# A fused attention and mixture kernel on one core: new orders for all engines, first queries loaded in another shape, and small edits to the softmax and to the last tile

## The chip, the cores and the metric

The kernel runs on one core of one Trainium2 chip, as one program and one launch. Its time is the device time of one execution in microseconds (us); three executions were timed. Besides those, one execution was recorded by the profiler, and every row shown below comes from that one.

A core has five engines, each working through its own list of instructions in order: TensorE (PE in the profile, with its weight loads as PEld), VectorE (DVE), ScalarE (ACT), GpSimd (POOL) and SyncE (SP). SP only issues transfers here; ACT and POOL issue a few of their own.

## The reference

The attention output of four batches is the token matrix of a two-layer network whose activation is a ratio of two polynomials.

```python
k_sum = k.reshape(B, H, nb, 32, D).max(axis=3)           # B=4, H=8, S=768, D=64
v_sum = v.reshape(B, H, nb, 32, D).mean(axis=3)
scores_l = where(|i-j| < 16, scale * q @ k.T, -1e9)      # a band
scores_s = scale * q @ k_sum.T + log(32)                 # one column for each block of 32 keys
a = softmax(concat(scores_l, scores_s))
x = a @ concat(v, v_sum)                                 # -> 3072 tokens x 512
h = x @ w_in                                             # 512 -> 2048
g = (a0 + a1*h + a2*h^2 + a3*h^3) / (1 + |b0|*|h| + |b1|*h^2 + 1e-6)
out = g @ w_out                                          # 2048 -> 512
```

## The kernel before

**The two halves.** The 3072 tokens are 48 windows of 64 queries (`jj`); eight windows make a group of 512 tokens, so there are six groups. A window of queries sees 96 neighbouring keys and 24 block maxima, 120 columns in all. For each window PE makes scores (`sc`), DVE the row maxima (`sm`), ACT the exponentials (`ss`), POOL the division by the row sum, PE a transpose (`pt`, copied to `pts`), and PE the product with the values (`av`), which ACT or DVE splits into a high part `xh` and a rest `xl`. From the third group on, the transposes go through DRAM (`cross`).

**The two layers.** A step is one group and one of 16 slices (`fc`) of the 2048 hidden columns: 96 steps. `h` of a step is 12 products of 128x512 on PE (high and low parts of tokens and weights), then a chain over ACT and DVE (`tq`, `ta`, `tu`) makes the activation's high part `gh` and, by a last product on POOL, its rest `gl`. Three steps later PE multiplies them by the slice of `w_out` into four sums `po`, 12 products again. PE can never do less than these 96 times 24 products.

**The weights.** A slice of both weight matrices arrives as one 1 MB transfer `wr`, 16 in all, and must be cut into a high and a low part before its `h`. `w_split` does this by one of several recipes, a letter in `MODE`: all have a pass of ACT, one of POOL and one of DVE over the raw words. Then mode `c` copies the high part on ACT and subtracts it on DVE; mode `e` copies on ACT, negates on ACT, and adds the raw words by an accumulating transfer that POOL issues.

**The first group.** Its eight windows take their queries from `qres` and keys from `kres`, resident tiles loaded at the start. Their block means of the values (`vs`) are made on PE, by products with a small averaging matrix, from all ten tiles of values of batch 0 (`vr`, `vw`, `vf`, `vlast`); the means are then copied into each window's value tile (`vw<-vs`, `vr<-vw`, `vlast<-vw`), so no `av` can begin before the last value tile has landed. `PATH` says how a window of the first two groups makes its maxima: `A` scales the maxima with a small DVE instruction and lets ACT read the scores from PSUM; `B` subtracts on DVE.

**What sets the order.** Every instruction is written down by one long list, `ORDER`: a token such as `h12` emits a whole step's products, `a5` the next stage of window 5, `w6` the next stage of the split of slice 6, `W6` its load, `P15` a second-layer step, `g12` the next stage of a step's chain. A wrapper (`Kept`) makes each engine follow the text of this list, and since it records every operation, nearly all instructions carry the line 162. `SLOTS` names the buffer of each tile. Transfers of SP and ACT use eight completion counters in turn: the ninth waits until the first has landed. `NWARM` = 6 products on zeros keep PE working until the first scores; `FILL` could add unread products elsewhere, and is empty.

Of the kernel before, what the change touches and what calls it, by code (L numbers as in the profile page):

```python
# [8 lines left out]
F32 = mybir.dt.float32  # L9
# [5 lines left out]
ALU = mybir.AluOpType  # L15
AX = mybir.AxisListType
# [7 lines left out]
P = 128  # L24
# [28 lines left out]
BYDVE = 'C2 C3 C4 C6 X0 X2 X3'  # L53
# [5 lines left out]
SLOTS = {'wm': '1010', 'ta': '01101010101010101010101010101010101010101010101010101010101010101010101010101010101010101101010101', 'tq': '01010101010101010101010101101010101011001010101010101101010101010101011010010101010101010010101010', 'st': '010101010101010101010101', 'gh': '012020120120120120120120120120120120120120120120121021021021021021021021020120120120120120120210210210', 'h': '0101011110101010101010101010101010010110100100101010101011010101001010101001001010110010101011010110101100101010100101010', 'ks': '0101', 'o': '01230130213021301320132013201320132013201', 'gl': '0121021021021021021021021021021021021021021021021021021021021021021021021021021021021021012102102102', 'sm': '012302312031203102310213021301230132103210321023', 'p': '0132103210123012301021302020232132302103013201021212131032010213013010121321202301021310101013020301021302130', 'xl': '0101010', 'a': '010010101001010101110010101010010111010000010010010111100001101111010010001010011011101000100010101010010100010101010101010101010', 'tu': '010101010101010101010101010101010101010101010101010101010101010101010101010101010101010101101010101', 'xh': '0110101', 'pts': '010101011011011010101011010101010101011011010101', 'vs': '01'}  # L59
NROW = 96  # L60
PTP = 'hhhhhhhhaaaaaaaa'
AVP = 'ooooooooaaaaaaaa'
# [6 lines left out]
K1 K0 K3 d1 S d0 K2 d2 B Q0 d3 c Q1 b0 a1 a0 a1 b2 k8 a0 W0 a2 b1 a2 w0 W1 V2 a1 w0 a0 a1 a3 a3 a2 a2 a6 w0 w1 a3 a4 I w1 W2 a3 V6 a2 a4 w2 a0 F w2 k9  # L69
V3 b3 a5 V1 a3 V0 V7 a4 v3 a2 w1 a6 a3 v1 a4 a6 v9 V5 V4 w1 a5 w0 v2 A8 w0 a0 a0 v6 v8 v0 a7 a6 v4 v5 v7 w1 w2 A9 a6 w1 a1 w2 m0 a5 a5 w2 a1 a7 m3 a0  # L70
b4 m4 W3 a4 w0 m1 a0 a3 a0 m7 a7 m6 a4 a1 a5 W5 w3 m2 W4 a1 G a4 a9 a5 a7 V8 a3 w3 a4 a2 a3 a7 a6 a1 w5 m5 a2 w2 a6 a4 W6 a7 w5 w3 a6 a5 a8 a6 a5 a5
A11 a7 w3 a2 a7 a7 w4 w4 w3 w3 h0 a9 w4 h1 w5 n2 w4 n3 g0 g0 w4 g0 a9 L10 q0 q0 g1 g0 g0 q1 n1 q1 a9 n5 n0 w4 g0 n4 a8 w5 a8 w5 a8 h2 V9 w5 g2 M g1 q2
h3 W8 a9 g2 g1 q2 a8 a9 A10 h4 a8 w6 W7 g2 w6 g1 g1 w6 o a8 a9 D10 L13 a8 P3 w6 w6 a8 g2 g2 g1 a9 g3 w8 g2 w6 g4 V10 W9 a9 q3 g3 w8 g3 b5 w7 q3 a11 P4
a11 w9 w7 q4 g4 g3 g3 W10 g3 q4 g4 a10 D13 a11 h5 w7 P5 w9 a10 L11 g4 h6 w8 g5 g4 w8 L12 w10 w7 g4 P6 w9 P7 D11 V11 q5 A13 D12 q5 g6 g5 w9 w10 w7 a10
a11 w7 g5 a10 g6 w8 h7 q6 a11 A12 g5 w9 a11 k13 a10 a10 a11 g5 a11 a10 a10 w8 g6 k12 w9 a11 W11 a10 q6 b6 g5 w10 g6 g6 g7 g7 W12 q7 w11 w10 w10 g6 g7
q7 a13 a13 A14 h8 A15 g7 g8 w12 a12 w11 P8 g7 h9 g8 w12 q8 w10 g7 w11 w11 q8 w12 g9 P9 W15 g9 g8 P10 a12 g8 h10 g8 w12 g8 w11 b7 a12 g9 q9 w11 q9 g9
w12 g10 W13 g9 P11 a15 h11 w12 V12 g9 w15 q10 a15 W14 a13 g10 P12 w13 a12 w13 g10 a13 V13 a14 q10 g10 A17 h12 g11 g11 w13 a13 g10 q11 w13 w13 g11 a12
w14 q11 g10 a15 a13 P13 w13 a14 w14 g11 a12 g12 g11 g11 a13 a13 g12 V15 q12 a13 a15 g12 h13 g13 P14 a14 w14 q12 a15 g13 w14 g12 a15 a14 a12 a14 w14
w14 g12 h14 q13 a12 a14 a12 a15 q13 V14 g12 w15 g14 a14 a15 a14 g13 w15 a15 w15 w15 P15 A16 a14 q14 g14 w15 g13 b8 q14 A18 g13 a17 g14 g13 h15 A19 a17
g14 g14 g15 g15 g15 q15 a16 q15 h16 P16 g14 g16 g15 a16 g15 g16 P17 h17 q16 L21 g15 P18 q16 g16 g16 g17 f0 a17 g16 q17 g16 a17 f0 g17 a16 g17 q17 g17  # L80
# [30 lines left out]
h93 q92 g92 q92 g92 g93 g93 g92 P93 g92 h94 q93 g93 q93 P94 g93 g93 g94 g94 q94 g94 g93 h95 q94 g95 g94 P95 P96 g95 g94 g95 g94 q95 q95 g95 g95 P97  # L111
g95 P98 f5 f5 f5 f5
"""
MODE = 'ccgcacccbceheccc'
NHALF = NT // HQ


@with_exitstack
def tile_kernel(ctx, tc, qw_in, kraw, kwin, vpad, vred, wio, a, b, cmask, cident, cavg, chot, cbias, out):
    nc = tc.nc  # L120
    class Slotted:


        taken = {}

# [639 lines left out]
```

## Time and profile before

| what | value |
|---|---|
| time, median of 3 runs (lowest to highest) | 633.04 us (632.68 to 633.34) |
| time of the profiled execution | 634.05 us |
| its span, first to last instruction | 632.1 us |
| PE busy | 613.5 us, 97% of the span |
| DVE busy | 558.3 us, 88% |
| ACT busy | 453.6 us, 72% |
| POOL busy | 249.5 us, 39% |
| mean granted PE clock | 0.989 |

The profiled execution has 1.95 us around its span and is 1.01 us above the median. Busy time on PE counts overlapped products, so it says where PE had something to do, not how fast it was. [...]

### The profile page before, as it was taken

The numbers are of one execution on the slowest core, as the hardware profiler recorded it, in microseconds if no ns is written. First come the engines' busy times: TensorE is split into PE (matmuls) and PEld (weight loads), VectorE is DVE, ScalarE is ACT, GpSimd is POOL, SyncE is SP. The second block draws the span as 40 slices with busy tenths as digits, with TensorE's granted clock in tenths as the row PEclk, the third lists the DMA queues.
The fourth block names the chain that finished last, engine by engine and source line by source line (L and its number), as shares of the span: only waits on it lengthen the run. The fifth ranks groups of instructions, "written<-read, shape, count | busy, mean of one in ns | idle before, by whom it ended". The sixth has DMA issues, their size and how long they took to land.

```text
span 632.1 us, 12059 instructions
## 1 busy us (share of the span) xinstructions
PE 613.5 (97%) x4188; PEld 492.6 (78%) x4188; DVE 558.3 (88%) x1073; ACT 453.6 (72%) x1007; POOL 249.5 (39%) x350
## 2 busy tenths in 40 slices
PE   8689989999999999999999999999999999999997
PEld 4477768777888888888888888887888888888885
DVE  5889999999888999989998799998978987798795
ACT  2898979877678767775876777777865875765653
POOL 0865465752416424224433233344242352122231
PEclk9599999999999999999999999999999999999999
DMA  8999668712334343334463413244423022100001
GB/s 317 268 335 319 234 207 275 183 47 68 105 118 147 121 138 91 120 99 146 114 200 114 156 49 113 82 136 125 136 80 101 26 84 87 67 0 2 0 1 66
DMA packets 52660, 80.25 MB, mean 127 GB/s; under 512 B 6440, under 2 KB 33736, under 8 KB 50680
## 3 DMA queue, kind: packets, MB, share of 16 engines
q1 hardware_dynamic: 51096, 75.00, 37.4%
q0 software_dynamic: 1280, 4.39, 3.0%
q8 instruction: 33, 0.54, 0.4%
q14 instruction: 27, 0.22, 0.1%
q10 hardware_dynamic: 224, 0.09, 0.1%
HBM read 60.33 MB, written 14.75 MB: 119 GB/s over the span
## 4 chain that ended last, share of the span: by engine, by line
PE 73%; DVE 12%; DMA 5%; ACT 4%; issue 2%; POOL 2%; SPq 1%; POOLq 0%; DVEq 0%; ACTq 0%
PE h L162 33%; PE po L162 33%; DVE tu L162 3%; DVE tq L162 3%; PE sc L162 3%; PE av L162 3%; DMA wr<-in_wio_dram 2%; DMA vr<-in_vpad_dram 2%; ACT ta L162 2%; DVE gh L162 2%; DVE wr L162 1%; POOL ss L162 1%; POOL gl L162 1%; DMA kres<-in_kraw_dram 1%; PE vs L162 1%
## 5 line engine op out<-in xcount | busy, mean ns | idle before, releaser
L162 POOL TENSOR_TENSOR gl<-tu,ta 128x512 fp32r<-128x512 f32 x96 | 132.6, 1382 | 327.5 <-DVE tu L162 221.8
L162 PE MATMUL po<-w,gh 128*128 128x512 f32 x384 | 119.7, 393 | 0.0
L162 PE MATMUL po<-wearly,gh 128*128 128x512 f32 x384 | 119.5, 392 | 0.0
L162 PE MATMUL h<-xh,wearly 128*128 128x512 f32 x384 | 97.1, 392 | 1.3 <-ACT xh L162 1.1
L162 PE MATMUL h<-xh,w 128*128 128x512 f32 x384 | 97.3, 392 | 0.0
L162 POOL TENSOR_SCALAR ss<-ss,sm 128x120 f32<-128x120 f32 x184 | 83.8, 473 | 23.0 <-DVE sm L162 22.3
L162 ACT ACTIVATE ta<-tq,cs 128x512 f32<-128x512 f32 x96 | 69.4, 723 | 31.9 <-DVE tq L162 29.5
L162 DVE SCALAR_TENSOR_TENSOR gh<-tu,cs,ta 128x512 fp32r<-128x512 f32 x96 | 74.8, 782 | 16.2 <-ACT ta L162 12.4
L162 PEld LDWEIGHTS h<-xh,wearly 128*128 128x128 f32 x384 | 71.4, 188 | 17.8 <-DVE tu L162 1.4
L162 PEld LDWEIGHTS h<-xh,w 128*128 128x128 f32 x384 | 71.3, 188 | 16.0 <-DVE tu L162 0.5
L162 PEld LDWEIGHTS po<-wearly,gh 128*128 128x128 f32 x384 | 71.5, 188 | 15.4 <-issue 0.6
L162 PEld LDWEIGHTS po<-w,gh 128*128 128x128 f32 x384 | 71.2, 188 | 15.4 <-issue 0.6
L162 ACT ACTIVATE ta<-h,cs 128x512 f32<-128x512 f32 x95 | 64.8, 682 | 22.1 <-POOL gl L162 21.8
L162 DVE SCALAR_TENSOR_TENSOR tu<-tu,cs,tq 128x512 f32<-128x512 f32 x96 | 74.0, 771 | 3.4
L162 ACT ACTIVATE sq<-h 128x512 f32<-128x512 f32 x72 | 42.0, 583 | 48.4 <-PE h L162 32.3
L162 PE MATMUL po<-wearly,gl 128*128 128x512 f32 x192 | 75.1, 391 | 0.6 <-POOL gl L162 0.6
L162 PE MATMUL po<-w,gl 128*128 128x512 f32 x192 | 75.2, 392 | 0.3 <-POOL gl L162 0.2
L162 ACT ACTIVATE tu<-h,cs 128x512 f32<-128x512 f32 x96 | 74.6, 777 | 0.0
L162 DVE SCALAR_TENSOR_TENSOR tu<-tu,cs,h 128x512 f32<-128x512 f32 x96 | 71.2, 743 | 1.8
L162 DVE SCALAR_TENSOR_TENSOR tq<-tq,gh 128x512 f32<-128x512 f32 x96 | 69.9, 729 | 1.8
L162 DVE TENSOR_TENSOR tu<-tu,h 128x512 f32<-128x512 f32 x96 | 65.1, 678 | 5.3 <-ACT tu L162 5.3
L162 ACT ACTIVATE ta<-ta 128x512 f32<-128x512 f32 x96 | 60.8, 634 | 3.0
(99 smaller groups left out, 903.6 us busy)
## 6 DMA issues: line engine op xcount, KB each, us to landing
wr<-in_wio_dram SPq DMA_DIRECT2D x15, 1024.0 KB, 5.5
cross<-tb SPq DMA_DIRECT2D x32, 256.0 KB, 2.1
vw<-in_vpad_dram SPq DMA_DIRECT2D x42, 192.0 KB, 2.8
kw<-in_kwin_dram SPq DMA_DIRECT2D x40, 192.0 KB, 3.3
out_dram<-o SPq DMA_DIRECT2D x24, 256.0 KB, 2.6
pts<-cross SPq DMA_DIRECT2D x96, 64.0 KB, 2.6
qw<-in_qw_dram SPq DMA_DIRECT2D x40, 128.0 KB, 2.9
kr<-in_kraw_dram SPq DMA_DIRECT2D x12, 384.0 KB, 4.3
```

Of the source, the lines that this page charges most:

```text
L162: out = getattr(self.engine, name)(*args, **kw)
```

## The change

`ORDER`, `SLOTS` and some of the tables that go with it are replaced as a whole. Their texts tell a reader nothing, so two lines of them stand here and the instructions that they produce stand further down.

```diff
-BYDVE = 'C2 C3 C4 C6 X0 X2 X3'
+BYDVE = 'C2 C3 C4 C6 X0 X13 X2 X3 X6'
-AVP = 'ooooooooaaaaaaaa'
+AVP = 'oohoaoooaaaaaaaa'
-MODE = 'ccgcacccbceheccc'
+MODE = 'ccgcaceebcehpccc'
-K1 K0 K3 d1 S d0 K2 d2 B Q0 d3 c Q1 b0 a1 a0 a1 b2 k8 a0 W0 a2 b1 a2 w0 W1 ...
+K1 Q0 K0 K3 S K2 W0 w0 d3 d0 w0 d1 d2 b0 a1 a0 Q1 a1 w0 W1 a1 a0 w0 ...
...
-        sync.dma_start(out=qres[:, lo:hi], in_=qw_in[0, lo:hi].rearrange("j p r q -> p j r q"))
+        sync.dma_start(out=qres[:, lo:hi], in_=qfirst[:, lo:hi])
...
-            first_q(*((0, 4), (4, HPG))[n])
+            first_q(*((0, 2), (2, HPG))[n])
...
-            dve.tensor_reduce(sm[:, 0, :], flat, axis=AX.X, op=ALU.max, negate=True)
+            peak = sc[:, NPAIR * NK:NPAIR * (NK + 1)] if path == "A" else sm[:, 0, :]
+            dve.tensor_reduce(peak, flat, axis=AX.X, op=ALU.max, negate=True)
             if path == "A":
-                dve.tensor_scalar_mul(sm[:, 0, :], sm[:, 0, :], SCALE)
+                dve.tensor_scalar_mul(sm[:, 0, :], peak, SCALE)
...
-        for pr in range(NPAIR):
-            (dve if jj in SSV else gps).tensor_scalar(ss[:, pr, :], ss[:, pr, :], sm[:, 1, pr:pr + 1], 1.0, op0=ALU.mult, op1=ALU.mult)
+        if jj in SSV:
+            dve.tensor_tensor(ss, ss, sm[:, 1, :].unsqueeze(2).broadcast_to((P, NPAIR, NK)), op=ALU.mult)
+        else:
+            for pr in range(NPAIR):
+                gps.tensor_scalar(ss[:, pr, :], ss[:, pr, :], sm[:, 1, pr:pr + 1], 1.0, op0=ALU.mult, op1=ALU.mult)
...
-            if mode in "cda":
-                dve.tensor_tensor(wt[:, 1, s], w, wt[:, 0, s], op=ALU.subtract)
+            if mode in "cdap":
+                (gps if mode == "p" else dve).tensor_tensor(wt[:, 1, s], w, wt[:, 0, s], op=ALU.subtract)
...
-        gps.tensor_tensor(gl, tu, ta, op=ALU.mult)
+        (dve if (g, fc) == (NG - 1, NFC - 1) else gps).tensor_tensor(gl, tu, ta, op=ALU.mult)
...
+            if g == NG - 1 and t == TPG - 1:
+                half = slice(0, DM // 2), slice(DM // 2, DM)
+                act.copy(o[:, half[0]], pos[g][t][:, half[0]])
+                act.dma_start(out=rows[:, half[0]], in_=o[:, half[0]])
+                dve.tensor_copy(o[:, half[1]], pos[g][t][:, half[1]])
+                sync.dma_start(out=rows[:, half[1]], in_=o[:, half[1]])
```

In words: the queries of the first group come from an input that is laid out as they are read, two windows first and six later, where before it was four and four in pieces of 1 KB. On path `A` (13 windows) the maxima are left in unused columns of the score bank and scaled from there. Windows 3 and 5 (`SSV`) are divided by one DVE instruction in place of four. Weight slices 6 and 7 go from mode `c` to `e`, slice 12 from `e` to a new `p`, which subtracts on POOL. The `xh` copies of windows 6 and 13 go from ACT to DVE. The last step's `gl` is made on DVE, and the last output tile is copied and stored in two halves by two engines and two queues. The first loads are also put in another order, W0 (the first weight slice) before the second part of the queries and ahead of everything else on ACT.

ACT's list from its first instruction, before (`ss`, `sm`, `sc` with a window's number; `wr0` is the first raw weight slice):

```order
L173 ACT_TABLE_LOAD
L195 DMA hot_94<-in_chot_dram 96x128
L196 DMA bias_95<-in_cbias_dram 96x360
L162 ACTIVATE ss1_187,sm1_188<-sc1_153,sm1_188 128x120 x4
L162 ACTIVATE sm1_188<-sm1_188 128x4
L162 ACTIVATE ss0_191<-ss0_191 128x4x120
L162 ACTIVATE ss2_240,sm2_241<-sc2_202,sm2_241 128x120 x4
L162 ACTIVATE sm2_241<-sm2_241 128x4
L162 ACTIVATE wr0_238<-wr0_238 128x1024
```

The same place of ACT in the changed kernel:

```order
L173 ACT_TABLE_LOAD
L195 DMA hot_94<-in_chot_dram 96x128
L196 DMA bias_95<-in_cbias_dram 96x360
L162 ACTIVATE wr0_138<-wr0_138 128x1024
L162 ACTIVATE ss1_182,sm1_183<-sc1_148,sm1_183 128x120 x4
L162 ACTIVATE sm1_183<-sm1_183 128x4
L162 ACTIVATE ss0_186<-ss0_186 128x4x120
L162 CAST wearly_105<-wr0_138 128x1024
L162 ACTIVATE wr1_197<-wr1_197 128x1024
```

The pass over the first weight slice has moved from behind three windows' exponentials to the head of the list, and its high copy (`wearly`) and the pass over the second slice follow ahead of the third window.

PE's list where the block means are made, before (`pt` a transpose, `vs0` the means of batch 0, `av0` the first product with values):

```order
L162 MATMUL vs0_402<-vr0_116,kres_108 32x128 x4
L162 MATMUL pt0_445<-ident_92,ss0_191 120x128 x4
L162 MATMUL vs0_402<-vlast_120,kres_108 32x128 x4
L162 MATMUL vs0_402<-vf0_4_348,kres_108 32x128 x4
L162 MATMUL vs0_402<-vw0_102,kres_108 32x128 x4
L162 MATMUL vs0_402<-vr2_118,kres_108 32x128 x4
L162 MATMUL vs0_402<-vr3_119,kres_108 32x128 x4
L162 MATMUL vs0_402<-vlast_120,kres_108 32x128 x4
L162 MATMUL pt6_487<-ident_92,ss6_312 120x128 x4
L162 MATMUL pt1_493<-ident_92,ss1_187 120x128 x4
L162 MATMUL av0_519<-pts0_450,vw0_102 64x64 x8
```

The same place of PE in the changed kernel:

```order
L162 MATMUL pt0_398<-ident_92,ss0_186 120x128 x4
L162 MATMUL vs0_403<-vr2_118,kres_108 32x128 x4
L162 MATMUL vs0_403<-vr3_119,kres_108 32x128 x4
L162 MATMUL vs0_403<-vlast_120,kres_108 32x128 x4
L162 MATMUL vs0_403<-vw0_102,kres_108 32x128 x4
L162 MATMUL vs0_403<-vr1_117,kres_108 32x128 x4
...
L162 MATMUL vs0_403<-vw1_103,kres_108 32x128 x4
L162 MATMUL vs0_403<-vf0_4_315,kres_108 32x128 x4
L162 MATMUL pt2_481<-ident_92,ss2_289 120x128 x4
L162 MATMUL av0_495<-pts0_463,vw0_102 64x64 x8
```

Before, 16 of the 40 products of the means stood ahead of the transpose of window 0 and 24 behind it; now all 40 stand together, and no transpose lies between them.

POOL's list around the splits of weight slices 6 and 7, before (`gl0_4` is the rest of step 4's activation; a DMA row is a transfer that POOL issues):

```order
L162 TENSOR_SCALAR wr6_654<-wr6_654 128x1024
L162 TENSOR_TENSOR gl0_1_730<-tu0_1_759,ta0_1_757 128x512
L162 TENSOR_TENSOR gl0_2_815<-tu0_2_820,ta0_2_818 128x512
L162 TENSOR_SCALAR wr8_843<-wr8_843 128x1024
L162 TENSOR_SCALAR wr7_881<-wr7_881 128x1024
L162 TENSOR_TENSOR gl0_3_842<-tu0_3_942,ta0_3_940 128x512
L162 TENSOR_SCALAR wr9_956<-wr9_956 128x1024
L162 DMA w8_1088<-wr8_843 128x1024
L162 TENSOR_TENSOR gl0_4_877<-tu0_4_951,ta0_4_949 128x512
L162 TENSOR_SCALAR wr10_1014<-wr10_1014 128x1024
```

The same place of POOL in the changed kernel:

```order
L162 TENSOR_SCALAR wr6_754<-wr6_754 128x1024
L162 TENSOR_SCALAR wr7_761<-wr7_761 128x1024
L162 TENSOR_TENSOR gl0_2_826<-tu0_2_829,ta0_2_827 128x512
L162 DMA wearly_105<-wr6_754 128x1024
L162 TENSOR_SCALAR wr9_834<-wr9_834 128x1024
L162 TENSOR_SCALAR wr8_850<-wr8_850 128x1024
L162 TENSOR_TENSOR gl0_3_901<-tu0_3_905,ta0_3_903 128x512
L162 DMA w8_1089<-wr8_850 128x1024
L162 TENSOR_TENSOR gl0_4_944<-tu0_4_965,ta0_4_963 128x512
L162 DMA wearly_105<-wr7_761 128x1024
L162 TENSOR_SCALAR wr10_1096<-wr10_1096 128x1024
```

Two accumulating transfers (`wearly<-wr6`, `wearly<-wr7`) have come in, one behind `gl0_2`, one behind `gl0_4`, and slice 7 is worked on ahead of slice 8.

## Rows read from the trace of the kernel before

**Rows 1.** Busy time by stretch: length, then PE, PEld, DVE, ACT, POOL, clock, DMA.

```profile
42.58:145.00 102.42, 97.80 (x689) 76.98 (x690) 99.10 (x149) 87.35 (x173) 55.89 (x64) 1.00 0.67 207
145.00:624.00 479.00, 478.50 (x2933) 391.06 (x2933) 425.24 (x851) 337.46 (x744) 168.25 (x246) 1.00 0.30 93
```

**Rows 2.** The chain that ended last, 150 to 160 us: start, length, what.

```profile
156.90 2.72 PE po L162 x12
```

**Rows 3.** The same chain from 0 to 46 us.

```profile
6.05 8.45 DMA wr<-in_wio_dram
...
30.17 1.83 PE vs L162 x48
...
32.02 0.25 ACT vw L162
...
33.74 1.39 ACT ss L162 x8
...
41.24 1.02 ACT wearly L162
42.26 0.28 ACT xh L162
...
42.58 3.07 PE h L162 x12
```

**Rows 4.** Moved by transfers, 40 slices of 0.85 us from 0 to 34 us.

```profile
GB/s 0 0 146 275 382 418 407 375 285 271 280 360 388 451 405 414 434 424 277 287 278 334 379 249 239 275 240 229 202 229 248 251 219 202 245 321 375 398 405 395
```

**Rows 5.** Busy time by stretch, columns as in rows 1.

```profile
17.00:27.00 10.00, 5.45 (x74) 3.78 (x75) 8.20 (x20) 8.89 (x34) 8.56 (x15) 0.50 1.05 263
27.00:30.70 3.70, 3.68 (x48) 2.47 (x52) 3.67 (x7) 3.67 (x12) 3.70 (x5) 0.50 1.06 249
30.70:42.60 11.90, 10.29 (x227) 8.11 (x219) 10.72 (x27) 10.45 (x28) 9.43 (x14) 1.00 1.02 392
```

**Rows 6.** Timeline, 12 to 16 us: start, length, instruction, idle before and releaser.

```profile
12.74 0.17 DVE L162 TENSOR_SCALAR sm<-sm 128x4 f32<-128x4 f32 x1
...
14.58 1.14 POOL L162 TENSOR_SCALAR wr<-wr 128x1024 int32<-128x1024 uint8 x1 [14.13 <-DMA wr<-in_wio_dram]
...
14.87 0.87 DVE L162 TENSOR_SCALAR sm<-sm 128x4 f32<-128x4 f32 x1
```

**Rows 7.** DVE's groups, 8 to 145 us: busy, mean ns of one, idle before.

```profile
L162 DVE TENSOR_REDUCE sm<-sc 128x4 f32<-128x480 f32 x16 | 10.3, 646 | 2.7 <-PE sc L162 2.7
...
L162 DVE TENSOR_TENSOR wearly<-wr,wearly 128x1024 fp32r<-128x1024 f32 x7 | 8.6, 1227 | 0.0
...
L162 DVE TENSOR_SCALAR sm<-sm 128x4 f32<-128x4 f32 x16 | 6.1, 383 | 0.6
...
L162 DVE TENSOR_TENSOR ss<-sc,sm 128x480 f32<-128x480 f32 x3 | 2.0, 657 | 0.1
L162 DVE TENSOR_REDUCE sm<-ss 128x4 f32<-128x480 f32 x3 | 1.9, 635 | 0.0
...
L162 DVE TENSOR_SCALAR ss<-ss,sm 128x120 f32<-128x120 f32 x8 | 1.7, 279 | 0.0
...
L162 DVE CAST xh<-av 128x256 fp32r<-128x256 f32 x3 | 1.3, 417 | 0.0
```

**Rows 8.** What SP waited for, 30 to 145 us: total, times, longest.

```profile
SPq L162 <- DMA wearly<-wr: 12.2, 1, 12.2
```

**Rows 9.** Timeline of the end, 618 to 632 us, columns as in rows 6.

```profile
620.48 0.68 DVE L162 TENSOR_TENSOR tu<-tu,h 128x512 f32<-128x512 f32 x1
...
624.52 1.29 POOL L162 TENSOR_TENSOR gl<-tu,ta 128x512 fp32r<-128x512 f32 x1 [2.49 <-DVE tu L162]
...
625.17 0.61 PE L162 MATMUL po<-w,gh 128*128 128x512 f32 x2
...
625.86 0.50 PE L162 MATMUL po<-w,gl 128*128 128x512 f32 x1
...
628.45 0.69 DVE L162 COPY o<-po 128x512 f32<-128x512 f32 x1 [0.67 <-PE po L162]
```

More of the change, by code (lines that the diff above doesn't have):

```diff
@@ L296, in unused @@
         for _ in range(FILL.get(what, 0)):
-            pe.matmul(bank[:, 0:P], ident, ident, start=True, stop=True, skip_group_check=True)
+            pe.matmul(bank[:, 0:NPAIR * NK], hot, bias[:, 1, :].unsqueeze(1).broadcast_to((NROW, NPAIR, NK)), start=True, stop=True, skip_group_check=True)
     def early_scores(n):
@@ L507, in w_split @@
         wt = weights(fc)
-        whole = [(s, w) for s, w, *_ in cooked] if mode in "cd" else [(slice(0, 2), packed.bitcast(F32))]
+        whole = [(s, w) for s, w, *_ in cooked] if mode in "cdp" else [(slice(0, 2), packed.bitcast(F32))]
         for s, w in whole:
-            if mode in "cef":
+            if mode in "cefp":
                 act.copy(wt[:, 0, s], w)
@@ L589, in finish @@
             o = pp.tile([P, DM], F32, tag="p", name=f"o{g}_{t}")
-            (dve.tensor_copy if g == NG - 1 and t % 2 else act.copy)(o, pos[g][t])
-            sync.dma_start(out=out[g * GT + t * P:g * GT + (t + 1) * P, :], in_=o)
+            rows = out[g * GT + t * P:g * GT + (t + 1) * P, :]
+            if g == NG - 1 and t == TPG - 1:
[4 more added lines that the diff above has]
+                sync.dma_start(out=rows[:, half[1]], in_=o[:, half[1]])
+            else:
+                (dve.tensor_copy if g == NG - 1 and t % 2 else act.copy)(o, pos[g][t])
+                sync.dma_start(out=rows, in_=o)
             yield
@@ L672, in tile_kernel @@
         elif kind in "vn":
-            b, total = (0, HPG + 2) if kind == "v" else (1, NJ // 2)
-            if b not in seen:
-                seen[b] = banks[VSP[b]].tile([P, 512], F32, tag=VSP[b], name=f"vs{b}"), 0
-            av, i = seen[b]
-            value_average(av, i, *(fv[1][n] if b else half_rows(n) if n < HPG else fv[0][n - HPG]), total)
-            seen[b] = av, i + 1
+            batch, total = (0, HPG + 2) if kind == "v" else (1, NJ // 2)
+            if batch not in seen:
+                seen[batch] = banks[VSP[batch]].tile([P, 512], F32, tag=VSP[batch], name=f"vs{batch}"), 0
+            av, i = seen[batch]
+            value_average(av, i, *(fv[1][n] if batch else half_rows(n) if n < HPG else fv[0][n - HPG]), total)
+            seen[batch] = av, i + 1
         elif kind == "m":
```

98 lines of the change are left out of this document (49 added, 49 removed).

## The prediction

> **What bounds the kernel now.** I first read busy time by stretch, to see where PE has nothing to do. From 145 to 624 us PE is busy for 478.50 of 479.00 us at full rate [rows 1], and a group of 12 products takes 2.72 us there, 0.227 each [rows 2]. Nothing in that long middle can be gained by another order; it can only be lost. Between 42.58 us, where the first step's products begin, and 145 us PE is busy for 97.80 of 102.42 us, so it idles for 4.62 us [rows 1], and DVE is busy for 99.10 of the same 102.42: there DVE sets the pace, and PE's waits are what it hands on. So the time is made of three pieces that can move: how late step 0 begins, those 4.6 us, and the end.
>
> For the beginning I read the chain that ended last [rows 3]. It runs over transfers until the block means can be finished: the first weight slice is issued at 6.05 and lands at 14.50, and the last products of the means end at 32.00. Then ACT carries it almost alone, from the copies of the means (32.02) to the last `xh` copy (42.54), and step 0 starts at 42.58. The transfer rates say how full the road is: about 410 GB/s in the good slices, 271 to 285 in the three from 6.8 us, where the queries move in 1 KB pieces, and 200 to 280 from about 19 to 29 us [rows 4]. In that time PE is at the lower of its two clock levels: 0.50 granted from 17 to 30.7 us. It idled for almost half of the stretch from 17 to 27, then worked for 3.68 of 3.70 us, and from 30.7 it has the upper level again, with 10.29 busy of 11.90 us until step 0 [rows 5].
>
> **The change part by part.** *Queries.* The same bytes in pieces of 2 and 6 KB. If the three slow slices ran at 410, they would save 2.55 x (1 - 279/410) = 0.8 us, and the two at 360 and 388 another 0.15: I take 1.0 us off all that lands later, the last value tile among it. Bounds: nothing, and 1.6 if the shape also helps what is queued behind.
>
> *Order at the start.* W0 now heads ACT's list, so the first exponentials wait for a landing. It no longer has 1 MB of queries ahead of it but 0.25 MB; 0.75 MB less at 410 GB/s is 1.8 us, so it lands near 12 to 12.7 us where it was 14.50, and its pass on ACT ends near 13.5. The first scaled maximum was there at 12.91 [rows 6]; I count the half microsecond as nothing, since the chain at this time is the transfers' [rows 3]. Behind ACT's wait stand all exponentials, so if W0 landed as late as before, the start would be 2.5 us later.
>
> All 40 products of the means now stand together on PE. They end when the last tile lands: 32.0 less 1.0. After them ACT has one window of exponentials more (1.39) and one copy of a weight slice less (1.02), two smaller copies less (0.28 for one); I count -0.2 [rows 3]. So ACT would release step 0 by 1.2 us earlier.
>
> But PE now has no dense stretch before the means are done. Before, PE worked almost without a stop from 27.0 us on, and the rate rose at 30.7 [rows 5]. In the new list the stretch like that one begins at about 31.0, 4.0 us later; if the rise moves with it, it comes at 34.7. Work in that time is done at half rate: 2.0 us lost on PE, of which its 1.6 us of waits before step 0 can take a part [rows 5]. Between 0.4 and 2.0 I take 0.6, near the low end, since ACT and not PE ends the chain there. Step 0: -1.2 + 0.6 = -0.6 us. Bounds: -1.6 and, with the rate low all the way, a loss that the second rival prices.
>
> *DVE's work up to step 15.* Scaling a maximum took 0.17 us when POOL was still, and 0.87 when it ran beside a POOL pass over raw weights [rows 6]; 16 of them took 383 ns in the mean [rows 7]. Reading PSUM, I take 0.17 for 13 of them: 13 x 0.213 = -2.8. Two subtractions of weight slices go: 2 x 1.227 = -2.5. Eight divisions of 0.279 become two of 0.657: -0.9. Two `xh` copies come: 2 x 0.417 = +0.8 [rows 7]. The seven tiny coefficient instructions, which stood in a wait for the queries, now come later; at 0.17 each they cost +1.2 at most. Together -4.2 us for an engine that is 97% busy. ACT gets two negations for slices 6 and 7 and loses one for slice 12 and two `xh` copies; it is not the bound there, 87.35 of 102.42 us [rows 1].
>
> [...] The rows that compare the two memories on DVE are reductions of the same shape: 646 ns from PSUM and 635 from SBUF [rows 7], so I leave the price of PSUM out. [...]
>
> How much of 4.2 us of relief reaches PE? At most the 4.62 us that it idles [rows 1]. I take half, -2.3 us: the new list brings waits of its own. Slices 6 and 7 now need an accumulating transfer, and the raw buffers of slices 10 and 11 come free only after it. Bounds: -4.6 and +1.5 (below).
>
> *The end.* POOL's last product ends at 625.81 and PE takes it up at 625.86; PE's two products before it began at 625.17, so at 0.227 each it could go on at 625.62. On DVE the product takes 0.68 as its like does, and is done by 625.2: -0.24 us. The last copy, 0.69 us for 512 columns, becomes two of 256 side by side (0.417): -0.27 [rows 7, 9]. The second queue's issue lies beside the first's. Sum -0.5; bounds 0 and -0.6. The division on DVE and slice 12's subtraction on POOL are in the sums above or on an engine with half its time free (55.89 of 102.42) [rows 1].
>
> Sum against the profiled execution: 634.05 - 0.6 - 2.3 - 0.5 = 630.65 us. That execution is 1.01 above the median of the runs, so the median to expect is 633.04 - 3.4 = **629.6 us**.
>
> **The rivals.** *Everything pays.* The rate returns as early as before, and DVE's relief removes all of PE's waits: -1.6 - 4.6 - 0.5 = -6.7, 626.3 us. For it: DVE's relief is almost as large as the waits [rows 1, 7]. Against: PE's dense stretch does begin later.
>
> *PE's clock comes back only in step 0 (slower).* If scattered products do not bring the upper level back, the 10.29 us of PE's work before step 0 become 20.6, less 1.6 us of waits: +8.7, less 1.2 for the transfers, and step 0's products run at half rate for some 2 us more. With the other gains that is +9.5 - 2.3 - 0.5 = +6.7, 639.7 us. It decides if the return comes after about 42 us: half of (42 - 30.7) less 1.6 eats the 4.0 us of the other gains. For it: in the 5.45 busy microseconds from 17 to 27 the rate did not return [rows 5]. Against: the products from 30.7 on, of the same kinds, kept it. [...]
>
> *The relief of DVE comes back as waits for transfers (same).* Before, SP stood 12.2 us until one such accumulating transfer of a weight slice had freed its buffer [rows 8]. With two more, slice 7's behind `gl0_4` on POOL, step 7 or slice 11's load may be late. Then PE's waits grow by 1.5 us in place of shrinking by 2.3: -0.6 + 1.5 - 0.5, 633.4 us.
>
> *The later part is worse.* Only 0.5 us of idle time lies from 145 to 624 us now [rows 1]; a list made anew may hold more. From 3 us on it takes the whole gain: 633 to 635 us.
>
> **How the numbers follow.** The forecast has 0.42, with its own range 627.5 to 631.8. Everything pays: 0.20. Waits for transfers: 0.18, about a quarter of it still faster, half the same. Late clock: 0.10. Later part worse: 0.10, half of it slower. About 0.2% (1.3 us) is what a measurement of this kernel can tell from no change. Faster: 0.42 + 0.20 + 0.05 = 0.67; same: 0.09 + 0.05 = 0.14; slower: 0.04 + 0.10 + 0.05 = 0.19. The range reaches from just below the best case to the upper end of the waits: 625.5 to 634.0 us.
>
> **What would show it.** Step 0's first products near 42.0 us; a granted clock that is 1.00 again by 35 us; 13 scalings near 0.17 us; PE's idle time from step 0 to 145 us near 2.3; no wait of PE for POOL's last `gl`, and a last copy of 0.42. I am wrong if the clock stays at 0.50 up to step 0, if PE waits for a weight slice in steps 6 to 11, or if 145 to 624 us holds more than 1 us of idle time.

## The result and the profile after

The changed kernel is not faster: in a first series of executions it is slower by half a per cent, in a second no difference is shown. Nine executions have a median of 636.74 us (633.77 to 643.24) beside 633.14 us of the kernel before, ratio 1.0052 [1.0027, 1.0077] (in brackets the 95% interval). A second series of twelve has a median of 635.95 us (631.34 to 642.34) beside 634.07, ratio 1.0007 [0.9978, 1.0037]; this ratio leaves the two longest (641.37 and 642.34) out as disturbed, though by what follows they may be the kernel's own. The forecast was 629.6 us, and no execution came that low. What is new is the spread. It goes with the mean granted clock that each execution reports, a share of PE's full speed; the traces of both kernels have 1.00 and 0.50 and no other level (number of executions: median, lowest to highest):

```
mean clock       changed kernel, 21 executions      kernel before, 151 executions (five series)
0.980 to 0.985   7: 641.37 (636.74 to 643.24)       2: 635.72, 636.19
0.986 to 0.990   7: 637.79 (633.77 to 639.40)      92: 633.92 (631.49 to 638.72)
0.991 to 0.995   7: 632.55 (631.34 to 636.54)      57: 632.78 (630.96 to 634.35)
```

Two things need a cause: why the changed kernel so often is in the upper lines, and why it gains nothing even in the last.

The profiled execution is one of the quicker ones: 635.33 us, span 633.2, clock 0.986. Its busy time by stretch (columns as in [rows 1] and [rows 5]):

```profile
17.00:27.00 10.00, 8.68 (x174) 6.66 (x170) 8.96 (x21) 9.85 (x41) 8.50 (x12) 0.59 0.99 288
27.00:30.70 3.70, 2.26 (x56) 1.43 (x48) 3.46 (x10) 2.11 (x10) 3.70 (x8) 1.00 1.02 365
30.70:42.60 11.90, 10.87 (x182) 8.47 (x182) 10.20 (x21) 10.05 (x34) 9.05 (x15) 0.86 1.02 349
42.58:145.00 102.42, 98.35 (x661) 75.95 (x662) 98.35 (x150) 85.85 (x163) 59.85 (x67) 1.00 0.66 202
145.00:624.00 479.00, 477.58 (x2957) 389.62 (x2957) 424.54 (x851) 338.20 (x746) 167.31 (x245) 1.00 0.31 94
```

Against [rows 1], PE's idle time from step 0 to 145 us went from 4.62 to 4.07 us where I forecast 2.3, and the long middle idles for 1.42 us where it idled for 0.50. The clock has another course, in stretches cut at its changes:

```profile
11.50:25.10 13.60, 12.85 (x236) 9.69 (x238) 11.35 (x29) 12.47 (x42) 8.69 (x14) 0.50 1.04 344
25.10:32.00 6.90, 4.42 (x98) 2.77 (x90) 6.65 (x15) 5.10 (x26) 6.50 (x10) 0.99 0.96 337
32.00:35.40 3.40, 3.40 (x36) 2.44 (x38) 2.53 (x7) 2.75 (x11) 3.25 (x7) 0.50 0.98 405
```

It falls at 11.5 us, returns at 25.1, falls again at 32.0 after a stretch in which PE was busy for 4.42 of 6.90 us, and returns at 35.4: 17.0 us at the lower level, where before it was 13.7 (17.05 to 30.70).

Of DVE's groups from 8 to 145 us these answer to [rows 7] and to the edits:

```profile
L162 DVE TENSOR_REDUCE sc<-sc 128x4 f32<-128x480 f32 x13 | 8.5, 654 | 2.5 <-PE sc L162 2.5
...
L162 DVE TENSOR_TENSOR w<-wr,w 128x512 fp32r<-128x512 f32 x2 | 2.4, 1234 | 0.0
L162 DVE TENSOR_SCALAR sm<-sc 128x4 f32<-128x4 f32 x13 | 2.1, 161 | 0.8
...
L162 DVE TENSOR_TENSOR ss<-ss,sm 128x480 f32<-128x480 f32 x2 | 1.4, 709 | 0.1
L162 DVE TENSOR_SCALAR cs<-coef 128x6 f32<-128x6 f32 x1 | 1.1, 1100 | 0.0
```

The scaling costs 161 ns, as forecast. But other DVE instructions are longer than before: the first of the coefficients took 1100 ns (161 before), and the two subtractions of slice 15 took 685 and 1783 ns, 1234 in the mean (687 before).

What PE waited for from 42.58 to 145 us (total, times, longest):

```profile
PE h L162 <- DMA w<-wr: 2.7, 1, 2.7
PE po L162 <- POOL gl L162: 1.0, 2, 0.5
PE h L162 <- DVE xh L162: 0.8, 1, 0.8
```

The largest is one wait for slice 8, which was not there before. The chain of waits in that place (start, length, what) and the transfers issued about it:

```profile
82.04 2.21 POOL ss L162 x4
84.24 10.45 DMA w<-wr
94.69 0.04 issue
94.73 1.19 PE h L162 x4
```

```profile
84.24 0.87 POOL L162 DMA_DIRECT2D w<-wr  x1
...
84.60 0.33 SPq L162 DMA_DIRECT2D wr<-in_wio_dram  x1
```

Slice 8's accumulating transfer is under way for 10.45 us, beside the load of slice 11 that SP issues 0.36 us later. This load waits for the buffer of slice 7, and since the change slice 7 gives it back by an accumulating transfer of its own. That looks like the rival of transfers, at the slices that it named; m67c below tests it.

The end (columns as in [rows 9]):

```profile
625.59 0.69 DVE L162 TENSOR_TENSOR gl<-tu,ta 128x512 fp32r<-128x512 f32 x1
...
628.38 1.05 ACT L162 COPY o<-po 128x512 f32<-128x512 f32 x2 [0.77 <-PE po L162]
...
628.64 0.39 PE L162 MATMUL po<-w,gl 128*128 128x512 f32 x1
629.46 0.38 ACTq L162 DMA_DIRECT2D out_dram<-o  x1
629.47 0.42 DVE L162 COPY o<-po 128x256 f32<-128x256 f32 x1 [1.07 <-ACT o L162]
```

PE no longer waits for the last `gl`. But the halves do not stand side by side: DVE's waits until ACT's is done. From the end of PE's last product (628.64 + 0.39) to the end of the span it is 4.2 us, where it was 3.7: 0.5 us more.

### The profile page after: what moved, and what is told of

It reads as the page before. It is cut to its first block, busy times and chain, and to the rows that moved or that the text cites. A ratio compares the mean times of both kernels' runs of the same rounds, so it can differ in the third digit from the quotient of the medians.

```text
span 633.2 us, 12065 instructions
## 1 busy us (share of the span) xinstructions
PE 617.0 (97%) x4188; PEld 493.6 (78%) x4188; DVE 557.0 (88%) x1068; ACT 453.3 (72%) x1007; POOL 250.7 (40%) x351
## 4 chain that ended last, share of the span: by engine, by line
PE 73%; DVE 13%; ACT 4%; DMA 3%; POOL 3%; issue 2%; SPq 1%; DVEq 0%; POOLq 0%; ACTq 0%
PE po L162 34%; PE h L162 32%; DVE tu L162 4%; PE sc L162 3%; PE av L162 3%; DVE tq L162 3%; DMA w<-wr 2%; POOL ss L162 2%; ACT ta L162 1%; DVE wr L162 1%; DVE gh L162 1%; SPq L162 1%; DMA kres<-in_kraw_dram 1%; DMA pts<-cross 1%; DVE ks L162 1%
## 5 line engine op out<-in xcount | busy, mean ns | idle before, releaser
L162 POOL TENSOR_TENSOR gl<-tu,ta 128x512 fp32r<-128x512 f32 x95 | 128.9, 1358 | 326.2 <-DVE tu L162 227.4
L162 DVE SCALAR_TENSOR_TENSOR gh<-tu,cs,ta 128x512 fp32r<-128x512 f32 x96 | 76.9, 804 | 11.4 <-ACT ta L162 7.3
L162 DVE SCALAR_TENSOR_TENSOR tq<-tq,gh 128x512 f32<-128x512 f32 x96 | 68.6, 714 | 1.8
L162 DVE SCALAR_TENSOR_TENSOR tq<-sq,cs,ta 128x512 f32<-128x512 f32 x72 | 53.4, 743 | 13.6 <-ACT ta L162 13.5
```

The lines of the kernel that those rows point to most:

```text
L162: out = getattr(self.engine, name)(*args, **kw)
```

## The experiments

Unread products and the last tile's form change nothing in the result, nor do the modes of slices, which only say who copies and subtracts. Ratios are to the kernel before, timed alongside.

**The changed kernel again.** No edit.

> The changed kernel itself, a second time, for a second profile and for the granted clock beside each time. Theory A (clock): the loss is PE's lower clock level at the start, which lasts for a different time in each execution; then time follows the mean granted clock, executions at 0.980 stand 3 to 8 us above those at 0.986 to 0.992, and a profile at a lower mean clock shows more of the first 45 us at 0.50. Theory B (transfers): the loss is the wait of step 8 for slice 8 (3.07 us between its products in the first profile) and a wait for attention weights (1.21 us near 215.5); then these waits vary from profile to profile and the clock does not tell the times apart. Median 635 to 638 by both.

635.95 us, as above. Its profile is a longer execution (639.40 us, clock 0.990), and shows what makes one. First DVE's place in the chain, then the instructions there:

```profile
98.00 8.63 DMA w<-wr
106.64 0.02 issue
106.66 0.03 DVE w L162
```

```profile
97.73 1.65 SPq L162 DMA_DIRECT2D wr<-in_wio_dram  x3
98.00 0.60 POOL L162 DMA_DIRECT2D w<-wr  x1 [5.34 <-ACT sq L162]
...
106.66 0.69 DVE L162 TENSOR_SCALAR w<-w 128x1024 fp32r<-128x1024 f32 x1 [4.54 <-DMA w<-wr]
```

The same place in the first profile:

```profile
99.10 0.60 POOL L162 DMA_DIRECT2D w<-wr  x1 [3.94 <-ACT sq L162]
...
100.19 1.75 SPq L162 DMA_DIRECT2D wr<-in_wio_dram  x3
...
103.13 0.86 DVE L162 TENSOR_SCALAR w<-w 128x1024 fp32r<-128x1024 f32 x1
```

Slice 11 (mode `h`) is copied by a transfer of POOL (0.5 MB) and negated by DVE. In the first profile the copy was issued 1.1 us ahead of the first of three loads (2 MB in all), and DVE had it without a wait. In the second the first of these loads, of 1 MB, was issued 0.27 us ahead of the copy and the others 0.1 and 1.05 us behind it; the copy took 8.63 us, and DVE stood 4.54 us with all steps' chains behind it. PE then idles, and the clock falls:

```profile
107.00:113.00 6.00, 2.87 (x12) 1.77 (x11) 5.90 (x10) 3.76 (x7) 2.95 (x3) 1.00 0.88 190
113.00:116.30 3.30, 3.30 (x10) 2.55 (x9) 3.23 (x6) 3.27 (x13) 0.66 (x1) 0.50 0.61 163
```

So a low mean clock is partly an effect of a wait. Theory A was wrong to take it for the one cause.

**Unread products,** at one place, then at all.

```diff
-FILL = {}
+FILL = {'v0': 8}                                    # fill_v
+FILL = {'r1': 4, 'r2': 3, 'r3': 3, 'b4': 4, 'b5': 4, 'b3': 4, 't0': 3, 'v0': 8}   # fill_all
...
+            if n == 0:                              # early_scores, fill_all only
+                unused(warm, f"r{pr}")
```

> The changed kernel with 8 unread products (480 columns each) ahead of the first attention products, where PE stands idle for 2.08 us at 29.04 while the means are copied. Nothing of the result changes. Theory A: the second fall of the clock, 31.96 to 35.37, does not come; mean clock at least 0.986 in most executions, median 1 to 3 us below the changed kernel's, and the spread (9.5 us over nine executions) at most half. Theory B: PE's time at the start is hidden behind transfers and ACT; median the same within 1 us, or up to 0.5 us later, and the same spread.

> The changed kernel with unread products in all of PE's gaps of the start: 10 between the four parts of the first scores, 4 ahead of each of the next three pairs of scores, 3 ahead of the second block of transposes, 8 ahead of the first attention products. Nothing of the result changes. Theory A: the clock does not fall at 11.5 us, mean clock 0.995 or more, median 632 to 634 and a spread below 3 us. If the clock falls all the same, the 33 products cost up to 0.4 us each at half rate and the start is 3 to 6 us later: 638 to 643. Theory B: the median is that of the changed kernel or later, whatever the clock does.

fill_v: 634.28 us (631.28 to 640.94), ratio 1.0006 [0.9986, 1.0027]; the second fall still came (0.50 from 28.1 to 31.4). A miss for A. fill_all: 632.78 us (631.59 to 636.50), ratio 0.9994 [0.9976, 1.0012], clock 1.00 from 8 to 34 us. It holds the clock until 34 us (0.50 then for 3.4 us, and again at 95.6) and takes off 3 us, not more than to the level of the kernel before. Four executions still stood at 634.0 to 636.5.

**Undoing the transfers of slices 6 and 7.**

```diff
-MODE = 'ccgcaceebcehpccc'
+MODE = 'ccgcacccbcehpccc'
```

> The changed kernel with slices 6 and 7 subtracted on DVE again, as before the change (no accumulating transfer for them, no negation on ACT). Theory B: POOL's queue of transfers is two shorter, slice 8 is ready 2 to 3 us earlier, the wait of step 8 is gone, and DVE's two subtractions (2.5 us) cost less than that: median 1 to 2 us below the changed kernel's. Theory A: the executions spread as before and the median stays within 1 us or is later by up to 2.5 us, since DVE has that much more to do.

639.13 us (636.69 to 642.76), ratio 1.0096 [1.0068, 1.0125]: worse than the changed kernel. PE's wait for slice 8 stayed (2.6 us), and DVE waited 3.3 us for slice 11. B in this form falls: slice 8's transfer landed at 95.15 us without the two transfers too, where it landed at 94.69 with them. That the run is slower still fits a list that relies on the DVE time that these two slices give back; this was not tried by itself.

**Slices 8 and 11 copied by ACT,** one, the other, both; with and without unread products.

```diff
-MODE = 'ccgcaceebcehpccc'
+MODE = 'ccgcaceeecehpccc'   # fa_m8e (and FILL as in fill_all)
+MODE = 'ccgcaceebceepccc'   # fa_m11e (and FILL)
+MODE = 'ccgcaceeeceepccc'   # fa_m8e11e (and FILL), m8e11e (without)
```

> The changed kernel with all the unread products, and slice 8 split as slice 10 is: ACT copies it instead of a transfer of POOL, then negation on ACT and the accumulating transfer as before. Theory B (transfers): PE waits 2 to 3 us in step 8 for this slice in every trace of the changed kernel, because its copy is in flight for 3.3 us ahead of the rest; with the copy on ACT the wait shrinks to under 1 us, and the fast executions come 1 to 2.5 us lower than those with the unread products alone (631.6 to 632.5). Rival: DVE is the bound in steps 8 to 15 and PE waits for it a little later: change under 0.5 us. The slow executions (636.3 and above) stay, 3 or 4 of 12.

> The changed kernel with all the unread products, and slice 11 copied and negated by ACT, where POOL's queue copied it by a transfer and DVE negated it. In the second profile of the changed kernel DVE stood 4.54 us at 102 us for that transfer, which was issued 0.27 us behind 2 MB of loads and took 8.6 us; in the first it was issued 1.1 us ahead of them and took 3.2. Theory (race of two queues): without this wait on DVE the executions at 634 to 636.5 disappear; all between 631.3 and 633.5, spread under 2.5 us, median near 632.2. Rival (the clock at the start makes the spread): the same spread as with the unread products alone, 631.6 to 636.5.

> Unread products, slice 8 and slice 11 both copied by ACT. By the sum of the two theories: median 630 to 631.5, spread under 2.5 us, faster than the kernel before by 0.2 to 0.5%. If DVE is the bound from step 8 on: 631.5 to 632.5. ACT has 2 us more to do in 42 to 145 us, of which it is busy 86 of 102; if that is too much, 632.5 to 633.5.

> The changed kernel without unread products, with slices 8 and 11 copied by ACT. Tells the waits from the clock: if the spread of the changed kernel (631.3 to 643.2 in 21 executions) came from the transfers of slices 8 and 11, it falls to under 3 us and the median to 631 to 632.5. If the clock at the start makes it, executions at a mean clock of 0.980 still stand 3 to 6 us above those at 0.992, and the median stays at 634 to 636.

fa_m8e: 635.16 us (632.38 to 645.03), ratio 1.0025 [0.9999, 1.0051]. Slice 8's wait stays (2.6 us), so its copy was not what made it late; in the profile DVE waited 7.4 us for slice 11. fa_m11e: 632.47 us (631.46 to 636.09), 0.9988 [0.9969, 1.0006]. fa_m8e11e: 633.53 us (631.84 to 635.40), 0.9999 [0.9980, 1.0018]. m8e11e: 633.86 us (631.22 to 636.75), 1.0003 [0.9980, 1.0026].

With slice 11 off POOL's queue the long executions are gone, with or without unread products: the highest of the 36 is 636.75 us, and 10 of the changed kernel's 21 stand above that. The profiles with slice 11's copy in POOL's queue show a race (us; "ahead" is how long before the next load the copy was issued):

```
kernel               ahead           copy took       DVE waited
old list, five       1.49 to 2.40    2.93 to 3.63    0
changed              1.09            3.21            0
fill_all             0.56            3.73            0
m67c                 0.33            7.41            3.3
fill_v               -0.21           8.62            4.5
changed, again       -0.27           8.63            4.5
fa_m8e               -0.62           11.44           7.4
```

The four with a wait are executions of 638.3 to 645.0 us, the changed kernel's first and fill_all's are 635.3 and 636.3. That points to slice 11's race for most of the long ones. It isn't the only cause: fill_all, which keeps the copy, has none above 636.50 in twelve, mended_nofill below, which has no such copy, has an execution of 637.66 us, and the spreads here are 3.6 to 5.5 us where I expected 2.5 to 3. Copying slice 8 on ACT as well gains nothing.

**Slice 8 without any transfer,** subtracted on DVE or on POOL; slice 11 by ACT, unread products, last tile whole.

```diff
+MODE = 'ccgcaceecceepccc'   # fa_m8c11e
+MODE = 'ccgcaceepceepccc'   # fa_m8p11e
```

> Unread products, slice 11 copied by ACT, slice 8 copied by ACT and subtracted on DVE: slice 8 needs no transfer at all. The last tile is copied whole by DVE again. Theory (slice 8's accumulating transfer meets slice 11's load, which slice 7's transfer sets free): the 2 to 3 us wait of PE in step 8 is gone, DVE pays 1.2 us; median 630 to 631.5. Rival (DVE is the bound there anyway): PE's wait turns into waits for DVE and POOL of the same size, median 632 to 633. The end: from the end of PE's last product to the end of the span 3.7 us as before the change, if the halves are what made it 4.2.

> The same with slice 8 subtracted on POOL (2.43 us there for slice 12) in place of DVE, last tile whole. If DVE's time is what counts, 0.5 to 1 us faster than with DVE; if POOL's products (gl) are late by it, PE waits for them 1 to 2 us and it is no faster.

fa_m8c11e: 632.83 us (631.39 to 633.67), 0.9985 [0.9972, 0.9999], the narrowest of the series of twelve. PE's wait for slice 8 is gone, and one of 1.3 us for slice 11's accumulating transfer stands in its place: the time is the rival's, the next gate is a transfer again. fa_m8p11e: 634.21 us, 1.0019 [1.0005, 1.0033], because the subtraction stands ahead of `gl` on POOL:

```profile
PE po L162 <- POOL gl L162: 3.2, 2, 2.8
```

In both the span ends 3.7 us after PE's last product, as before the change: the halves cost 0.5 us.

**The old list with only the small edits.** before_relief has the maxima scaled from PSUM and the two divisions in one instruction; before_small has those, the queries from their own array (4 KB pieces), `gl` on DVE, and halves in two tiles; before_best has the relief and `gl`.

```diff
+            peak = sc[:, NPAIR * NK:NPAIR * (NK + 1)] if path == "A" else sm[:, 0, :]   # all three
...
+        (dve if (g, fc) == (NG - 1, NFC - 1) else gps).tensor_tensor(gl, tu, ta, op=ALU.mult)   # small, best
...
+        sync.dma_start(out=qres[:, lo:hi], in_=qfirst[:, lo:hi])   # small
...
+                o2 = mp.tile([P, DM // 2], F32, tag="tq", name="o_last")   # small
```

> The kernel before, with only two edits of DVE: 13 maxima written to PSUM and scaled from there (383 to 161 ns each, 2.9 us less), and the two divisions in one instruction each (0.8 us less). Same list, same transfers. My forecast's step that half of DVE's relief reaches PE would make it 1.5 to 2 us faster: 631.3 to 632. If the list's other waits take it: 633 to 633.6, no difference.

> The kernel before with all the small edits and its own list: the two of DVE, the queries from an array of their own in pieces of 4 KB, the last product gl on DVE, and the last tile in two halves that are two tiles, so that the second copy needn't wait for the first. Queries 0.5 to 1 us, relief 0 to 2, gl 0.24 to 0.46, halves 0.27: 629.5 to 631.5 if the old list passes them on; the clock of the old list (0.989 to 0.992) stays. If the start is bound by ACT and not by the queries, 632 to 632.7. The end: if the wait for the first half comes from the shared tile, the two copies stand side by side; if from PSUM, one behind the other again.

> The kernel before and its own list, with the two edits of DVE (maxima scaled from PSUM, two divisions in one instruction each) and the last product gl on DVE; queries and last tile as before. The two edits alone gave 632.19 against 633.42; gl is 0.24 to 0.46 more: 631.4 to 632.2, ratio 0.997 to 0.9985, if the gain is real. If it was chance: 633 to 633.5.

before_relief: 632.19 us, 0.9983 [0.9964, 1.0001]. before_best: 632.42 us (630.50 to 633.76), 0.9974 [0.9961, 0.9988]. before_small: 633.34 us, 0.9999 [0.9979, 1.0018]: it looks as if queries and halves together took away what the rest gains, but the last two intervals overlap. Its end, in two tiles:

```profile
627.13 1.05 ACT L162 COPY o<-po 128x512 f32<-128x512 f32 x2 [0.77 <-PE po L162]
...
628.21 0.42 DVE L162 COPY o_last<-po 128x256 f32<-128x256 f32 x1 [1.07 <-ACT o L162]
```

The second copy still waits for the first; only the source in PSUM is shared now. Whether the program or the chip orders two readers of it was not tried. That the queries cost anything here is not shown: one profile has a wait of 1.2 us for keys at 323 us, which may be chance.

**Slice 11 by ACT, and unread products, in the old list.**

```diff
-MODE = 'ccgcacccbceheccc'
+MODE = 'ccgcacccbceeeccc'   # before_best11e, on before_best
...
+FILL = {'r1': 4, 'r2': 3, 'r3': 3, 'b4': 4, 'b5': 4, 'b3': 4, 't0': 3, 'v0': 8}   # before_fill, on before
```

> The same with slice 11 copied and negated by ACT. If the old list's spread at one clock comes from the same race (a transfer in POOL's queue against loads of 1 MB), executions above 634 disappear and the median is 0.5 to 1 us lower. If it comes from elsewhere, the spread stays at 4 to 5 us and ACT's 1 us more makes it no faster.

> The kernel before with the 33 unread products of the other runs at the same places of its list (other than its products for the means, which stand among the scores there). If the clock alone makes the time, it goes to 0.997 or more and the median 1 to 2 us below 633.4. If the old list has its start bound by transfers and ACT, the clock rises and the median stays within 0.5 us, or is later by up to 2 us where the products stand in PE's way.

before_best11e: 634.44 us, 1.0003 [0.9985, 1.0022]: 2 us above before_best. No profile of the old list shows DVE waiting for slice 11, so there is nothing to gain by it there; that ACT's copy is what costs is not shown. before_fill: 645.00 us (643.83 to 646.05), 1.0179 [1.0156, 1.0202], a miss: step 0 begins at 50.98, and the clock fell all the same, three times:

```profile
21.10:31.30 10.20, 7.98 (x94) 5.08 (x98) 6.50 (x19) 6.99 (x29) 6.78 (x12) 0.50 1.06 303
```

Unread products are no gain by themselves. They must fit into the gaps of the list that they are put in.

**The changed kernel mended,** and taken apart again: fa_m11e with the last tile whole, then without unread products, then without those among the first scores.

```diff
-MODE = 'ccgcaceebcehpccc'
+MODE = 'ccgcaceebceepccc'
...
+FILL = {'r1': 4, 'r2': 3, 'r3': 3, 'b4': 4, 'b5': 4, 'b3': 4, 't0': 3, 'v0': 8}   # after_mended
+FILL = {}                                                     # mended_nofill
+FILL = {'b4': 4, 'b5': 4, 'b3': 4, 't0': 3, 'v0': 8}          # mended_late
```

> The changed kernel with unread products, slice 11 copied by ACT, and the last tile whole again: fa_m11e less the halves. 632.47 less 0.45: 632.0, spread under 5 us, ratio to before 0.998. If it isn't below before_best, the new list itself gains nothing over the old one.

> The changed kernel with slice 11 copied by ACT and the last tile whole, without unread products. If slice 11's transfer makes most of the loss: median 632 to 633, no execution above 636, whatever the clock. If the clock at the start makes it: mean clocks of 0.980 to 0.992 again and a median of 634 to 636, 2 to 4 us above the same kernel with the products.

> The mended kernel with unread products ahead of the second to fourth pair of scores, the second transposes and the first attention products alone, none between the parts of the first scores. If the level is lost in PE's gaps of the first scores (8 to 12 us), the clock falls again near 11 to 21 us, the products run at half rate in PE's way, and the median is 1 to 3 us above the mended kernel's 632.0. If only the later gaps matter, it is the same within 0.7 us.

after_mended: 632.04 us (630.50 to 633.14), 0.9971 [0.9952, 0.9990]: faster than the kernel before and the changed one, and no faster than before_best (0.9974), which keeps the old list. mended_nofill: median 633.95, 1.0007 [0.9982, 1.0031]. mended_late: 632.58 us (629.87 to 635.03), 0.9992 [0.9972, 1.0012], within 0.7 us of after_mended, and in its profile the clock is 1.00 until 21.3 us. In mended_nofill the five executions at a clock of 0.981 to 0.987 take 634.0 to 637.7 us, the six at 0.989 to 0.995 take 629.7 to 633.9: without slice 11's race the clock still goes with the time, and one execution is above the 636 us that the expectation allowed. So the products point to 1 to 2 us once slice 11's race is gone, but the intervals of the three overlap. From 42.58 to 145 us after_mended has PE idle for 1.72 us:

```profile
42.58:145.00 102.42, 100.70 (x679) 78.01 (x675) 99.85 (x152) 89.81 (x171) 59.02 (x66) 1.00 0.67 204
```

## Why the prediction was wrong

By step 18 all have issued the same products (after_mended 33 unread ones more), so its first product tells what a start and the steps behind it are worth (us, from the profiles):

```
kernel           step 0   step 18   between
before           42.58    159.46    116.88
changed          42.79    159.26    116.47
changed, again   40.02    163.25    123.23
before_relief    41.15    157.46    116.31
before_best      42.10    158.35    116.25
mended_nofill    41.24    157.26    116.02
after_mended     43.39    157.24    113.85
```

**The start (-0.6).** The size was fair, in part by luck. The means' copies began at 30.81 where they began at 32.02 [rows 3], close to the time that I forecast, but not by its path. I had the means end at 31.0, when the last value tile lands; in the profile their last product ended at 28.72, and ACT came to the copies two microseconds later, because its own exponentials were late:

```profile
28.32 0.40 PE L162 MATMUL vs<-vf,kres 128*32 128x128 f32 x8
...
28.56 0.36 ACT L162 ACTIVATE ss<-sc,sm 128x120 f32<-128x120 f32 x1 [1.58 <-DVE sm L162]
...
30.81 0.53 ACT L162 COPY vw<-vs 24x128 f32<-24x128 f32 x2
```

In this profile step 0 began 0.21 us later than before. Step 0 in the six profiles of the new list without products among the scores (changed twice, fill_v, m67c, m8e11e, mended_nofill) lies at 40.02 to 42.79, with 41.2 in the middle; in the five of the old list without any at 41.15 to 42.58. The rise of the clock by 35 us came as forecast (35.4), by a way that I had not seen: up at 25.1 and down again. My single figure of 0.6 us for it hid that it differs between executions.

**DVE's relief (-4.2).** Mis-sized, and put in the wrong place. The scaling gave 3.1 us (16 x 0.383 less 13 x 0.161 and 3 x 0.326), the subtractions 2.4, the divisions 0.3 of busy time (1.7 to 1.4; the eight before overlap, and I had added up their lengths to 2.2). But from the beginning to step 18 DVE is busy for 143.30 us where it was 145.34, 2.0 less: 0.9 went to the first coefficient instruction (I had allowed 1.2 for all of them), 1.1 to slice 15's second subtraction, 1.1 to the packing of the slices (15 x 1330 ns, before 1254). And much of the relief lies ahead of step 0: ten of the 16 scalings and all the divisions, in both kernels. From step 0 to step 18 DVE is busy for 112.23 us where it was 113.08, only 0.85 less. A timeline row shows what lengthened the first coefficient instruction: it stands at 21.11 inside a POOL pass over raw weights.

```profile
20.39 1.79 POOL L162 TENSOR_SCALAR wr<-wr 128x1024 int32<-128x1024 uint8 x1 [0.28 <-DMA wr<-in_wio_dram]
21.11 1.10 DVE L162 TENSOR_SCALAR cs<-coef 128x6 f32<-128x6 f32 x1
```

This is the 0.87 us of [rows 6] again, on another instruction. I had priced the wait as the scaling's own. In both rows the DVE instruction ends within 0.03 us of the POOL pass (15.74 and 15.72, here 22.21 and 22.18), so I now take it for a wait for POOL, and other DVE instructions can be long beside POOL too: slice 15's second subtraction began at 143.19 beside a `gl` of POOL (142.84 to 144.42) and took 1783 ns, where the first took 685. Not all are. The scaling at 69.97, which reads PSUM, took 164 ns with 0.93 us of a POOL pass left, and a reciprocal at 81.52, which reads SBUF, 165 ns with 0.42 us left. What tells those that are long from those that are not, no run shows.

**"I take half, -2.3 us": the step that failed.** From step 0 to step 18 the changed kernel gained 0.41 us, and PE's idle time up to 145 us fell by 0.55. The share was not what failed: I took half of 4.2 us, a relief counted from 8 us on [rows 7], and set it against PE's idle time behind step 0 [rows 1], where only 0.85 us of relief lay. Half of that came through. On the old list (before_relief) DVE has 0.92 us less there, and PE gained 0.57. Nor were PE's waits mainly DVE's to give back: in the new list slice 8's accumulating transfer holds step 8 for 1.4 to 3.1 us in 11 of the 12 profiles that have it (not in after_mended's), whether slice 8 is copied by POOL or by ACT. In the profile before it landed at 94.02, and the last four products of step 8 began at 94.82 without a wait; in the changed kernel step 8 began 2.9 us earlier (89.95 against 92.88, with other products ahead of it), but the slice landed at 94.69 and the last four products began at 94.73. What PE had gained by then it gave back there. In before_relief PE already waits 0.6 us for the same slice. That is a wait of the kind that the rival of transfers named, but not by the two transfers that it blamed (m67c), and the loss went further than I priced it (633.4). The copy of slice 11, whose mode the change did not touch, went out 1.5 us or more ahead of the next load in the old list; now it is issued within about a microsecond of 2 MB of loads, and the order differs between executions. Where it comes too late, DVE stands (3.3 to 7.4 us in four profiles) and PE behind it, and in "changed, again" the clock fell after that (0.50 from 113.0). "Changed, again" took 6.8 us more from step 0 to step 18 than the first, most of it for this. I had looked for late transfers in front of PE, not for one that an in-order DVE waits for with every step behind it.

The copy of 0.5 MB that took 3.21 us in the first profile took 8.63 us in the second, where the first load was ahead of it; no run shows why it took that much longer.

**The clock as a rival (639.7 if it comes back after 42 us).** It did not come in that form: it was back by 38 us in all profiles of the new list. But a lower clock takes part in the loss, at the start and, in 8 of these 14 profiles, again at some time from 90 to 123 us, the stretch of the waits for slices 8 and 11. In "changed, again" the later fall stands behind the wait for slice 11: 0.50 from 113.0, after PE was busy for 2.87 of 6.00 us. The falls at the start of the first profile came after idle time as well: PE was busy for 2.20 of the 3.50 us before 11.5, and for 4.42 of the 6.90 before 32.0. From 11.5 to 25.1 us 0.50 was granted, and PE was busy for 12.85 of these 13.60.

**The end (-0.5).** `gl` on DVE was right: the wait of 0.24 us is gone. The halves have the wrong sign: DVE's 0.42 stands behind ACT's copy, and the end is 0.5 us longer, where I took -0.27. Together, from the start of PE's last twelve products to the end of the span, it is 7.06 us (626.14 to 633.2), before 6.93.

**The later part.** I named 145 to 624 us idle for more than 1 us as a sign of error; it is 1.42 us, most of it one wait of 1.0 us for attention weights from DRAM at 215 us.

The profiled execution adds up to: start +0.21, steps up to 18 -0.41, step 18 to the last products +1.17, end +0.13, in all +1.1 of span. The other executions add the race and the clock.

That after_mended, whose unread products put step 0 later by 2 us (43.39 against 41.24), reaches step 18 as early as mended_nofill goes with slice 8: mended_nofill's profile waits 2.6 us for it, in after_mended's the wait is 0.3.

What stays open: why slice 8's accumulating transfer takes 7.9 to 10.5 us in the new list where it took 6.2 to 7.9 in the old one; what sets the clock's course at the start, which differs between executions of one kernel; and where the spread at one clock level in the kernel before (631.5 to 638.7) comes from.

## What to carry to other kernels

When an order is remade, look for each transfer that an in-order engine waits for and ask which other transfers are issued within a microsecond of it: the mean of a profile hides a race that one execution wins and the next loses, so look at several profiles and at the spread before a median is explained. Time taken off a busy engine is worth only what lies in the stretch where others wait for it, and only what the next gate lets through; so sort the relief by stretch, and name that gate (here the transfers of slices 8 and 11), before a share of it is booked. Small edits are best timed on the old order: here three of them were worth 0.26% alone, and the changed kernel, which has them too, was not faster.

## What the runs showed of the hardware

Two small DVE instructions from SBUF to SBUF took as long as what was left of a POOL pass over raw weights beside them (coefficients: 0.16 us alone, 1.10 with 1.07 of the pass left; scaling: 0.17 and 0.87, with 0.85 left). The same scaling read from PSUM took 0.16 us with 0.93 left, and a reciprocal in SBUF 0.17 with 0.42 left. A 0.5 MB copy in POOL's queue took 8.63 us where a 1 MB load was issued 0.27 us ahead of it and 1 MB more within 1.05 us behind; issued 1.1 us ahead of all of them it took 3.21, and 0.33 us ahead 7.41. PE stayed at the lower clock level for 13.6 us in which it was busy for 12.85 (changed kernel, from 11.5 us). Copies of the two halves of one PSUM tile by ACT and DVE ran one after the other, with one destination tile (ACT until 629.43, DVE from 629.47) or with two (until 628.18, from 628.21).
